# Attention and a wide MLP on one core: the fourth pair's products of v, its finish and the first MLP groups sit some cycles earlier, and the opening's loads go head by head

## The chip, the cores and the metric

The kernel runs on one core of a Trainium2 chip. The metric is the device time of one execution in microseconds (us). The engines are TensorE (PE in the profile, PEld for its weight loads), VectorE (DVE), ScalarE (ACT), GpSimd (POOL) and SyncE, whose queue (SPq) issues the DMAs. Each engine runs its own instructions strictly in order.

## What is computed

Attention over 8 batches of 8 heads, 576 positions and 64 dimensions, where only scores within tau of their row's maximum are kept; then an MLP over the 4608 rows of 512 features that come out, with 2048 hidden features and a slope of alpha below zero.

```python
scores = scale * np.matmul(q, k.transpose(0, 1, 3, 2))
thresh = np.max(scores, axis=-1, keepdims=True) - tau
scores = np.where(scores >= thresh, scores, -1000000000.0)
scores = scores - np.max(scores, axis=-1, keepdims=True)
attn = np.exp(scores)
attn = attn / (np.sum(attn, axis=-1, keepdims=True) + 1e-09)
attn_out = np.matmul(attn, v)
...
x = attn_out.transpose(0, 2, 1, 3).reshape(B * S, H * D)
h = x @ w_in
g = np.maximum(h, 0.0) + alpha * np.minimum(h, 0.0)
out = g @ w_out
```

The weights w_in and w_out arrive as float64; everything else is float32.

## The kernel before

**Pairs and cycles.** The 64 heads are worked in 32 pairs (class `Pair`), four to a batch. A pair has nine units of 128 queries, and each unit is one *cycle* of the main loop: 288 cycles for attention, pair `pi` in cycles `9*pi` to `9*pi+8`. In cycle i VectorE masks unit i and sums its rows (`mask`, L430), TensorE makes the scores two units ahead (`scores`, L395) and transposes unit i (`turn`, L439; `turn_k`, L455, and L453 for the fifth unit, the tail), ScalarE takes exponentials (`expo`, L418) behind VectorE's row maximum (`rowmax`, L410), and the transposed blocks are copied out of PSUM (`hi`, `lo`). Scores have two PSUM buffers.

**Beside the softmax.** Everything else of a pair hangs on a table of cycles: `at_cycle(i, f)` puts a step into cycle i, and the steps of a cycle run in the order in which they were put there. `PREP` places loads, splits and moves of q, k and v; `AVW` and `AVS` the four products of v (`avmul`, L542, copied out by `avout`, L553); `FINW` and `FINS` the seven steps of the finish: reciprocals of the row sums (`recip`, L560), their transpose (`rturn`, L565), a copy to `rt` that goes through DRAM and comes back spread over the rows as `rb` (`rout`, L569 to L574), the sum of v (`fin_add`), the multiply by `rb` (`fin_mul`, L589, POOL), a compare for rows that kept nothing (`fin_un`, L592, VectorE) and the last add with the store of x into `xs` (`fin_out`, L595 and L596). The first four pairs, which are batch 0, are worked whole (`WHOLE = 4`) and use the W tables, the others are split into high and low parts and use the S tables. For whole pairs each product is issued in two parts in neighbouring cycles. The numbers in the tables count from the pair's first cycle; `PREP` counts from the cycle nine earlier.

**The MLP beside attention.** Of the 16 blocks of 128 hidden features, seven (`F1`) are worked during attention, in groups of 256 rows (`Mlp`). A group is ready in cycle i once its rows' batches are finished, which a constant stands for:

```python
while nready < len(groups1) and sum(groups1[nready]) <= (i - RDY) // (9 * NPAIR) * S:
```

From then on `Mlp.cycle` gives TensorE work up to 2.6 us a cycle by its own count (`room`): first the load of x (L174, split by L180 on ScalarE and L182 on POOL one cycle later), then from the third cycle on *hidden blocks* (12 matmuls of line 194; L206 and L207 follow on VectorE and ScalarE), not in cycles that hold a product of v, then *output matmuls* (line 224). What is left when attention ends is done in the *drain*, in the scheduler's order, beside the decoding of the other nine blocks' weights (`Split64`, L113 to L152); then comes the last phase over all rows (`phb`, `accb`).

**Weights.** The float64 words are turned into two float32 parts by a chain over ScalarE, VectorE and POOL. The pieces of the seven blocks are decoded in cycles -3 to 40.

**Order.** Inside attention the order on TensorE, ScalarE, VectorE and POOL is the one in which the code issues; the order on SyncE's queue, and all orders after attention, are the scheduler's.

**Opening.** The first pair's k and q come doubled, in eight loads: all of k, then all of q; then tau, a first piece of w_in, the second pair's k and q. VectorE negates tau (L796) and then splits k and q for both heads (`prep_first`, L318 to L322).

Of the kernel before, what the change touches and what calls it, by code (L numbers as in the profile page):

```python
# [28 lines left out]
# A float64's upper word read as a float32 orders values by magnitude. These two  # L29
# bounds are the words of the least normal float32 and of the largest one that  # L30
# still rounds to a finite 12-bit part.
# [29 lines left out]
RDY = 13  # L61
# [8 lines left out]
def tile_masked_attention_moe(  # L70
# [31 lines left out]
    class Split64:  # L102
        """float64 bits -> hi + lo in float32r, to 24 bits or better."""
# [140 lines left out]
    class Turned:  # L244
        """The transposed scores of two heads, in parts, with columns of ones that sum v."""
# [21 lines left out]
    class Pair:  # L267
        """The steps of two heads of one batch; each queues work on one or two engines."""
# [8 lines left out]
        def load(self, what):  # L277
# [11 lines left out]
            if pi == 0:  # L289
                # The first pair's are doubled on the way in, so that its scores start at once.  # L290
                r = ap1.tile([P, KW if what == "k" else 2 * S], F32, tag="vst" if what == "k" else "p", name=f"{what}r{pi}", bufs=2)
                for j in range(2):
                    n = w if j else S
                    for half in range(2):
                        nc.sync.dma_start(r[half * D : (half + 1) * D, j * S : j * S + n], src[j * D : (j + 1) * D, :n])
                if what == "k":
                    self.kr = r
                else:
                    self.qr = r[:, : 2 * S].rearrange("p (a b) -> p a b", a=2)
                return  # L300
# [9 lines left out]

        def prep_first(self, j):
            """The splits of q and k for one head, before there is other work."""
# [11 lines left out]
        # The two heads' q and k come one above the other. The parts are made so, and then moved:  # L324
        # qst holds the parts of q one above the other, kh and kl each part of k twice.
# [51 lines left out]
        # A unit is (chunk of queries, head), or the tail: the last queries of the  # L377
        # first head above the first queries of the second.
# [225 lines left out]
    def first_at_cycle(i, fn):  # L604
        soon.setdefault(i, []).append((fn, ()))

    # Where in a pair's nine cycles the work beside the softmax falls.
    for p in pairs:
        o = 9 * p.pi
        n = o - 9  # L610
# [346 lines left out]
```

## Time and profile before

| | |
|---|---|
| three timed runs | 1399.51, 1401.48 and 1401.74 us; median 1401.48 |
| the profiled execution | span of 1397.3 us from the first to the last instruction; its time as a whole isn't listed apart |
| mean granted clock of TensorE | 0.995 |
| attention's last products of v | 829.16 us |
| the last phase's first matmul | 947.71 us |

Each row of the profile's order of time gives start and duration in us, engine, line, operation, tiles (out<-in), shapes and a count of merged instructions; in brackets the idle time of the engine ahead of it and what ended that. Rows of the chain of waits have start, duration and what worked. In the page, the first part gives busy time, share of the span and number of instructions of each engine.

### The profile page before, as it was taken

The page shows a single profiled execution, that of the slowest core. Times are in us where ns is not written, and L with a number is a line of the kernel's source. Part 1 is how long each engine was busy: PE and PEld are TensorE (multiplying, and loading weights), DVE is VectorE, ACT ScalarE, POOL GpSimd, SP SyncE. Part 2 cuts the span into 40 slices and gives each one's busy share as a digit, 9 for nine tenths or more (in the row PEclk, how much of TensorE's full clock was granted, in tenths as well). Part 3 has the DMA queues.
Part 4 walks back from the last instruction along what each step waited for, and adds up shares of the span by engine and source line. Part 5 has one row for each costly group of instructions (what it writes and reads, how often), then busy time and mean ns, then how long its engine had stood idle before and what let it go on. Part 6 is the DMA issues. An engine that isn't in the chain of part 4 may idle for free.

```text
span 1397.3 us, 23301 instructions
## 1 busy us (share of the span) xinstructions
PE 1339.4 (96%) x8116; PEld 1181.2 (85%) x8116; DVE 975.7 (70%) x1933; ACT 820.9 (59%) x1843; POOL 762.3 (55%) x821
## 2 busy tenths in 40 slices
PE   5888899999999999999999999888999999999998
PEld 4556789999999999999999998777888888888887
DVE  6999988888888898898888957986323323323332
ACT  7788888888888888888888854453112012111100
POOL 3776676666676666576676557566434124223311
PEclk9999999999999999999999999999999999999999
DMA  8643634545545444454454214433320220111011
GB/s 249 184 127 106 180 105 122 162 116 142 147 117 150 139 134 131 132 154 127 128 160 132 83 57 153 132 109 128 121 74 17 91 91 33 59 61 42 19 61 38
DMA packets 94628, 157.67 MB, mean 113 GB/s; under 512 B 14160, under 2 KB 39024, under 8 KB 94512
## 3 DMA queue, kind: packets, MB, share of 16 engines
q1 hardware_dynamic: 94512, 156.19, 38.4%
q8 instruction: 65, 1.06, 0.3%
q14 instruction: 51, 0.42, 0.1%
HBM read 85.53 MB, written 28.46 MB: 82 GB/s over the span
## 4 chain that ended last, share of the span: by engine, by line
PE 80%; DVE 9%; ACT 4%; DMA 2%; issue 2%; POOL 2%; SPq 0%; DVEq 0%; POOLq 0%; ACTq 0%
PE phb L194 16%; PE accb L224 16%; PE s L395 10%; PE av L542 10%; PE acca L224 9%; PE pha L194 9%; PE t L439 7%; DVE p L430 2%; DVE nmx L410 2%; DMA wri<-in_moe_w_in_dram 1%; PE tk L455 1%; DVE wti L135 1%; POOL wi L152 1%; ACT xb L555 1%; ACT xa L553 1%
## 5 line engine op out<-in xcount | busy, mean ns | idle before, releaser
L410 DVE TENSOR_REDUCE nmx<-s 128x1 f32<-128x576 f32 x288 | 217.0, 753 | 72.6 <-PE s L395 69.5
L215 ACT ACTIVATE gb<-ptb 128x512 fp32r<-128x512 f32 x81 | 50.9, 630 | 337.7 <-DVE ptb L873 337.3
L218 POOL TENSOR_TENSOR gb<-ptb,gb 128x512 fp32r<-128x512 f32 x81 | 104.4, 1290 | 257.0 <-ACT gb L215 256.8
L224 PE MATMUL acca<-wo,ga 128*128 128x512 f32 x756 | 230.7, 419 | 7.2 <-ACT ga L215 4.0
L224 PE MATMUL accb<-wo,gb 128*128 128x512 f32 x972 | 221.9, 389 | 0.0
L224 PEld LDWEIGHTS accb<-wo,gb 128*128 128x128 f32 x972 | 182.4, 188 | 37.9
L430 DVE SCALAR_TENSOR_TENSOR p<-s,thr,p 128x576 f32<-128x576 f32 x256 | 206.6, 807 | 1.3 <-ACT thr L423 0.9
L194 PE MATMUL phb<-xh,wi 128*128 128x512 f32 x648 | 202.9, 392 | 1.1 <-ACT xh L180 1.1
L194 PE MATMUL pha<-xh,wi 128*128 128x256 f32 x1008 | 199.7, 284 | 3.7 <-DVE pta L873 3.4
L418 ACT ACTIVATE p<-s,nmx 128x576 f32<-128x576 f32 x256 | 190.0, 742 | 10.8 <-DVE nmx L410 10.5
L395 PE MATMUL s<-kh,qst 128*128 128x288 f32 x640 | 142.2, 312 | 38.1 <-DVE p L430 23.3
L194 PEld LDWEIGHTS pha<-xh,wi 128*128 128x128 f32 x1008 | 163.8, 190 | 9.9 <-DVE pta L873 4.6
L224 PEld LDWEIGHTS acca<-wo,ga 128*128 128x128 f32 x756 | 132.8, 191 | 28.6 <-ACT ga L215 5.3
L439 PE MATMUL t<-ident,p 128*128 128x128 f32 x1024 | 154.6, 274 | 0.0
L395 PEld LDWEIGHTS s<-kh,qst 128*128 128x128 f32 x640 | 101.4, 193 | 61.5 <-issue 29.4
L903 DVE TENSOR_TENSOR ob<-accb,pin 128x512 f32<-128x512 f32 x36 | 24.2, 689 | 181.9 <-PE accb L224 181.9
L194 PEld LDWEIGHTS phb<-xh,wi 128*128 128x128 f32 x648 | 122.6, 189 | 27.2 <-ACT xh L180 1.5
L194 PE MATMUL pha<-xl,wi 128*128 128x256 f32 x504 | 142.2, 282 | 0.0
L872 DVE TENSOR_SCALAR ptb<-phb,alpha_sb 128x512 f32<-128x512 f32 x81 | 60.7, 751 | 108.5 <-PE phb L194 96.4
L395 PE MATMUL s<-kl,qst 128*128 128x288 f32 x640 | 133.8, 299 | 0.0
L194 PE MATMUL phb<-xl,wi 128*128 128x512 f32 x324 | 127.2, 393 | 3.6 <-POOL xl L182 3.6
L439 PEld LDWEIGHTS t<-ident,p 128*128 128x128 f32 x1024 | 126.5, 141 | 0.1
(117 smaller groups left out, 2772.6 us busy)
## 6 DMA issues: line engine op xcount, KB each, us to landing
kr<-in_k_dram SPq DMA_DIRECT2D x31, 320.0 KB
rb<-rvd SPq DMA_DIRECT2D x64, 144.0 KB
xs<-xa SPq DMA_DIRECT2D x32, 288.0 KB
part<-po SPq DMA_DIRECT2D x36, 256.0 KB
pin<-part SPq DMA_DIRECT2D x36, 256.0 KB
out_dram<-ob SPq DMA_DIRECT2D x36, 256.0 KB
vr<-in_v_dram SPq DMA_DIRECT2D x28, 320.0 KB
qr<-in_q_dram SPq DMA_DIRECT2D x31, 288.0 KB
```

The lines of the kernel that those rows point to most:

```text
L194: nc.tensor.matmul(ph[:, :n], w[:, c, :], xx[:, c, :n], start=(c == 0 and ti == 0), stop=(c == NCC - 1 and ti == 2),)
L215: nc.scalar.activation(g[:, 0, :n], t[:, :n], AF.Copy)
L218: nc.gpsimd.tensor_tensor(g[:, 1, :n], t[:, :n], f(g[:, 0, :n]), op=ALU.subtract)
L224: nc.tensor.matmul(acc[:m, :], gg[:, g, o : o + m], w, start=(first and ti == 0), stop=(last and ti == 2))
L395: nc.tensor.matmul(ps[:, h, :288], w, kk[:, a + h * 288 : a + (h + 1) * 288], start=(ki == 0 and i == 0), stop=(ki == 1 and i == n - 1),)
L410: nc.vector.tensor_reduce(self.nmx[:, j : j + 1], self.S[u][0][:, :, :288], axis=AX.XY, op=ALU.max, negate=True)
L418: nc.scalar.activation(pj, ps[:, :, :288], AF.Exp, bias=nmx[:, j : j + 1], scale=1.0)
L430: nc.vector.scalar_tensor_tensor(pj, ps[:, :, :288], thr[:, j : j + 1], pj, op0=ALU.is_ge, op1=ALU.mult, accum_out=self.sm[:, c : c + 1])
L439: nc.tensor.transpose(tb[:, c, :], pt[:, j, j * D + c * P : j * D + (c + 1) * P], ident)
L542: nc.tensor.matmul(pa[:m, :n], w, x, start=(part == 0 and c == 0), stop=(part == z.parts[-1] and c == NKC))
L872: nc.vector.tensor_scalar(t[:, :n], ph[:, :n], 0.0, alpha_sb[:, fc : fc + 1], op0=ALU.min, op1=ALU.mult)
L903: nc.vector.tensor_tensor(ob[:m], acc[:m], pi_[:m], op=ALU.add)
```

## The change

The fourth pair, the last of batch 0, gets tables of its own (`AVL`, `FINL`). Its products of v are issued whole, in cycles 32, 34, 36 and 37, where they stood in two parts each in cycles 32 to 39. The steps of its finish stay where they were up to `rout`; the sum of v moves three cycles forward, the multiply and the compare three, the last add and the store four: all three of the latter are in cycle 40. A group of the MLP is ready from seven cycles earlier in the first two batches' time (`RDY` 6 instead of 13) and three earlier after that (10). In the opening the loads go k, q of head 0, then k, q of head 1, and tau's negative stands behind the four splits. Comments are taken out, which shifts line numbers.

```diff
-RDY = 13
+AVL = (5, 7, 9, 10)
+FINL = (9, 10, 11, 11, 13, 13, 13)
+RDY = (6, 10)
...
             if pi == 0:
-                # The first pair's are doubled on the way in, so that its scores start at once.
-                r = ap1.tile([P, KW if what == "k" else 2 * S], F32, tag="vst" if what == "k" else "p", name=f"{what}r{pi}", bufs=2)
-                for j in range(2):
-                    n = w if j else S
-                    for half in range(2):
-                        nc.sync.dma_start(r[half * D : (half + 1) * D, j * S : j * S + n], src[j * D : (j + 1) * D, :n])
...
+                self.load_first()
                 return
...
+        def load_first(self):
+            self.kr = ap1.tile([P, KW], F32, tag="vst", name=f"kr{self.pi}", bufs=2)
+            qr = ap1.tile([P, 2 * S], F32, tag="p", name=f"qr{self.pi}", bufs=2)
+            self.qr = qr.rearrange("p (a b) -> p a b", a=2)
+            for j in range(2):
+                for r, src, w in ((self.kr, k, S + j * D), (qr, q, S)):
+                    for half in range(2):
+                        nc.sync.dma_start(
+                            r[half * D : (half + 1) * D, j * S : j * S + w], src[0, 0][j * D : (j + 1) * D, :w]
+                        )
...
         fin = FINW if p.whole else FINS
-        if p.whole:
+        if p.pi == NPAIR - 1:
+            fin = FINL
+            for c, step, j in zip(AVL, (0, 0, 1, 1), (0, 1, 0, 1)):
+                at_cycle(o + c, p.avmul, step, j)
+                at_cycle(o + c + 1, p.avout, step, j)
+        elif p.whole:
...
         p.load("k")
-        p.load("q")
         nc.sync.dma_start(tau_sb, tau.partition_broadcast(P))
-        nc.vector.tensor_scalar(ntau_sb, tau_sb, -1.0, None, op0=ALU.mult)
...
         p.prep_first(0)
         p.prep_first(1)
+        nc.vector.tensor_scalar(ntau_sb, tau_sb, -1.0, None, op0=ALU.mult)
...
-            while nready < len(groups1) and sum(groups1[nready]) <= (i - RDY) // (9 * NPAIR) * S:
+            while nready < len(groups1) and sum(groups1[nready]) <= (i - RDY[i >= 18 * NPAIR]) // (9 * NPAIR) * S:
```

What this does to the engines' orders, at three places. In the listings each row is a line, an operation and its tiles; after the change a line's number is 2 higher in the helpers (L127 is L129, L194 is L196) and 5 higher in the steps of `Pair` (L319 is L324, L430 is L435, L592 is L597).

VectorE's queue at the opening, before the change (`ntau_sb` is tau's negative, `kl` and `qst` the low parts of k and q, `wti` the first weight):

```order
L796 TENSOR_SCALAR ntau_sb<-tau_sb 128x1
L319 TENSOR_TENSOR kl_201<-kr_181,kh_200 128x576
L322 SCALAR_TENSOR_TENSOR qst_110<-qr_186,qst_110 64x576
L319 TENSOR_TENSOR kl_201<-kr_181,kh_200 128x640
L322 SCALAR_TENSOR_TENSOR qst_110<-qr_186,qst_110 64x576
L127 TENSOR_SCALAR wti_212<-wti_212 128x512
```

and with the change:

```order
L324 TENSOR_TENSOR kl_200<-kr_181,kh_199 128x576
L327 SCALAR_TENSOR_TENSOR qst_110<-qr_182,qst_110 64x576
L324 TENSOR_TENSOR kl_200<-kr_181,kh_199 128x640
L327 SCALAR_TENSOR_TENSOR qst_110<-qr_182,qst_110 64x576
L811 TENSOR_SCALAR ntau_sb<-tau_sb 128x1
L129 TENSOR_SCALAR wti_212<-wti_212 128x512
```

The negative moved from ahead of the splits to behind them, still ahead of the weight.

VectorE's queue around cycles 41 to 43, before the change; the compare of the fourth pair (`rb`) stands behind the masks of units 5, 6 and 7 of the fifth pair (`p_2`, `p_3`):

```order
L495 TENSOR_TENSOR eo_115<-t_3_1469,eo_114 128x4x128
L430 SCALAR_TENSOR_TENSOR p_2_1487,sm_1294<-s_5_1458,thr_5_1485,p_2_1487 128x576
L410 TENSOR_REDUCE nmx_5_1484<-s_6_1491 128x1
L495 TENSOR_TENSOR tt_121<-tk_t,tt_120 64x64
L495 TENSOR_TENSOR tt_123<-tk_t,tt_122 64x64
L495 TENSOR_TENSOR eo_115<-t_4_1498,eo_114 128x4x64 x2
L410 TENSOR_REDUCE nmx_7_1553<-s_7_1518 128x1
L430 SCALAR_TENSOR_TENSOR p_2_1487,sm_1294<-s_6_1491,thr_5_1485,p_2_1487 128x576
L495 TENSOR_TENSOR eo_115<-t_5_1526,eo_114 128x4x128
L430 SCALAR_TENSOR_TENSOR p_3_1556,sm_1294<-s_7_1518,thr_7_1554,p_3_1556 128x576
L410 TENSOR_REDUCE nmx_7_1553<-s_8_1560 128x1
L592 TENSOR_SCALAR rb_1448<-rb_1448,vs_1531 128x576
```

and with the change:

```order
L500 TENSOR_TENSOR eo_115<-t_3_1475,eo_114 128x4x128
L597 TENSOR_SCALAR rb_1451<-rb_1451,vs_1454 128x576
L435 SCALAR_TENSOR_TENSOR p_2_1491,sm_1296<-s_5_1464,thr_5_1489,p_2_1491 128x576
L415 TENSOR_REDUCE nmx_5_1488<-s_6_1495 128x1
L500 TENSOR_TENSOR tt_121<-tk_t,tt_120 64x64
```

The compare moved ahead of the mask of unit 5 (cycle 41).

TensorE's queue in cycle 49, before the change (`s` are scores, `t` and `tk_t` transposes, `av` a product of v):

```order
L395 MATMUL s_6_1783<-kh_1313,qst_111 128x288 x2
L395 MATMUL s_6_1783<-kl_1315,qst_111 128x288 x2
L439 MATMUL t_4_1794<-ident,p_t 128x128 x4
L453 MATMUL tk_t<-ident,p_t 64x128
L395 MATMUL s_7_1815<-kh_1313,qst_111 128x288 x2
```

and with the change:

```order
L400 MATMUL s_6_1823<-kh_1315,qst_111 128x288 x2
L400 MATMUL s_6_1823<-kl_1317,qst_111 128x288 x2
L444 MATMUL t_4_1834<-ident,p_t 128x128 x4
L458 MATMUL tk_t<-ident,p_t 64x128
L196 MATMUL pha_2_1848<-xh_0_1617,wi_462 128x256
L196 MATMUL pha_2_1848<-xl_0_1619,wi_462 128x256
```

A hidden block (`pha`) of the first group now stands in this cycle, and so in cycles 45 and 48. Counted over the whole order, the first hidden block is in cycle 45 instead of 52. Hidden blocks and output matmuls done by the end of a cycle, before and after: 0 and 0 against 3 and 0 (cycle 51); 7 and 0 against 10 and 9 (cycle 63); 16 and 64 against 17 and 84 (cycle 89); 21 and 84 against 21 and 84 (cycle 99); 93 and 512 against 93 and 514 (cycle 286). In cycles 98 and 99 the changed order has neither; before they had two blocks and three output matmuls. SyncE's queue has the store of the fourth pair's x and the first load of x (L174) ahead of a later pair's load of q and moves of k, where they stood behind those moves.

More of the change, by code (lines that the diff above doesn't have):

```diff
@@ L289, in load @@
             if pi == 0:
-                r = ap1.tile([P, KW if what == "k" else 2 * S], F32, tag="vst" if what == "k" else "p", name=f"{what}r{pi}", bufs=2)
-                for j in range(2):
-                    n = w if j else S
-                    for half in range(2):
-                        nc.sync.dma_start(r[half * D : (half + 1) * D, j * S : j * S + n], src[j * D : (j + 1) * D, :n])
[L296 to L299, printed above, removed]
+                self.load_first()
                 return
```

## The prediction

> **What bounds the kernel now.** I read the page first, then the windows, then the order of time around the change, then the chain.
>
> ```profile
> span 1397.3 us, 23301 instructions
> PE 1339.4 (96%) x8116; PEld 1181.2 (85%) x8116; DVE 975.7 (70%) x1933; ACT 820.9 (59%) x1843; POOL 762.3 (55%) x821
> ```
>
> The three timed runs have a median of 1401.48 us; the profiled execution has no time of its own beside its span of 1397.3, so I put 4.2 us around the span, work in microseconds of the span and carry the difference over to the median. TensorE is the bound as a whole, but not everywhere. The windows (from, to and length, then the busy times of the engines PE, PEld, DVE, ACT and POOL, the granted clock, DMA share, GB/s; the odd limits are the first transposes of cycles 32 and 38, 43 and 52, 98 and 100):
>
> ```profile
> 107.17:125.69 18.52, 16.20 (x88) 10.53 (x87) 18.40 (x35) 15.01 (x34) 13.52 (x11) 1.00 0.54 141
> 138.39:160.44 22.05, 16.38 (x124) 15.25 (x123) 20.17 (x45) 19.99 (x47) 11.15 (x11) 1.00 0.58 157
> 190.00:200.00 10.00, 7.93 (x47) 7.53 (x47) 7.57 (x20) 7.79 (x17) 6.64 (x7) 0.83 0.73 201
> 250.00:300.00 50.00, 50.00 (x367) 47.73 (x366) 44.19 (x99) 43.43 (x104) 32.76 (x42) 1.00 0.51 142
> 291.43:297.04 5.61, 5.61 (x46) 5.51 (x45) 5.51 (x14) 5.16 (x12) 3.54 (x6) 1.00 0.87 246
> 890.00:900.00 10.00, 7.49 (x35) 5.86 (x34) 9.71 (x13) 4.79 (x9) 8.39 (x7) 0.90 0.45 135
> ```
>
> From 200 to 825 us TensorE has no gap: work taken out there is time won, as far as VectorE (44.2 of 50) lets the cycles shrink. In cycles 43 to 51 VectorE and ScalarE are the fuller ones and TensorE has 22.05 - 16.38 = 5.67 us free; in cycles 32 to 37 VectorE is full (18.40 of 18.52). Around 890 us VectorE decodes the late weights and binds.
>
> **The change part by part.** *Opening.*
>
> ```profile
> 5.82 0.58 SPq L795 DMA_DIRECT2D tau_sb<-in_tau_dram  x1
> 6.81 0.68 ACT L321 ACTIVATE qst<-qr 128x576 fp32r<-128x576 f32 x1 [1.85 <-DMA qr<-in_q_dram]
> 9.09 0.15 DVE L796 TENSOR_SCALAR ntau_sb<-tau_sb 128x1 f32<-128x1 f32 x1 [9.09 <-DMA tau_sb<-in_tau_dram]
> 11.07 0.69 ACT L123 ACTIVATE wti<-wri 128x512 f32<-128x512 f32 x1 [2.29 <-DMA wri<-in_moe_w_in_dram]
> 12.41 0.43 DVE L127 TENSOR_SCALAR wti<-wti 128x512 f32<-128x512 f32 x1
> ```
>
> VectorE sat until tau landed at 9.09, with the splits of k and q queued behind it. Now the four splits stand ahead of tau's negative, and q of head 0 is issued two transfers (some 1.3 us) sooner. By these rows all four can be done by some 10 us instead of 12.4. Next in VectorE's queue is L127, which needs ScalarE's L123, and that waits for a weight load whose place in the queue is unchanged: it ends at 11.07 + 0.69 = 11.76. So what is late next is the weight, and the gain is 12.41 - 11.76 = 0.65 us, between 0 (swallowed by a later DMA wait) and 0.65. I take **-0.65**.
>
> *The fourth pair's products of v.* Its four products were issued in two parts each, in cycles 32 to 39; now each is issued whole, in 32, 34, 36 and 37.
>
> ```profile
> 126.22 1.84 PE L542 MATMUL av<-eo,vst 128*64 128x322 f32 x6
> 128.83 0.76 DVE L410 TENSOR_REDUCE nmx<-s 128x1 f32<-128x576 f32 x1 [1.18 <-PE s L395]
> ```
>
> The product of 322 columns that leaves cycles 38 and 39 has ten matmuls, 10 x 1.84 / 6 = 3.1 us. It lands in cycles 32 to 37, where TensorE has 18.52 - 16.20 = 2.3 us free: 0.8 us uncovered. Behind it VectorE's wait of 1.18 us for scores goes, of which I credit 0.5, since VectorE is the bound there. Bounds: -0.5 (all covered) and +3.1 (nothing is). I take **+0.3**.
>
> *Its finish.* The chain is reciprocal row, write, read back by rows, multiply (POOL), compare (VectorE), add (POOL), store, reload as x. The end of the last pair shows it with nothing in the way:
>
> ```profile
> 831.59 0.27 ACT L569 ACTIVATE rt<-rp 9x128 f32<-9x128 f32 x1
> 837.05 1.21 POOL L589 TENSOR_TENSOR xa<-xa,rb 128x576 f32<-128x576 f32 x1 [2.88 <-DMA rb<-rvd]
> 838.29 0.52 DVE L592 TENSOR_SCALAR rb<-rb,vs 128x576 f32<-128x576 f32 x1 [10.40 <-POOL xa L589]
> 840.13 0.32 SPq L596 DMA_DIRECT2D xs<-xa  x1
> 841.64 3.78 SPq L174 DMA_DIRECT2D xr<-xs  x3
> 841.64 5.87 DMA xr<-xs
> 125.12 0.27 ACT L569 ACTIVATE rt<-rp 9x128 f32<-9x128 f32 x1
> 131.03 0.81 DVE L430 SCALAR_TENSOR_TENSOR p<-s,thr,p 128x576 f32<-128x576 f32 x1
> 139.09 0.74 ACT L328 ACTIVATE kh<-kr 128x640 fp32r<-128x640 f32 x1
> 143.65 0.67 ACT L345 ACTIVATE qst<-qr 128x576 fp32r<-128x576 f32 x1
> ```
>
> From the row of reciprocals to the multiply are 837.05 - 831.59 = 5.46 us, to the compare 6.70, to the store 8.54, to the reload 10.05. Counted from the fourth pair's own row at 125.12 the compare can start at 131.82. In VectorE's order it now stands right ahead of the mask that started at 131.03, and that mask, the next row maxima and the transposes behind them queue after it: 0.79 us of stall; the compare's own 0.5 us only moves. The store comes at 133.66 and the reload's issue at 135.2; a load of 512 KB takes 4.42 us (the weight load below), so x is there at 139.6. ScalarE splits it right behind L328, which ends at 139.83: just in time. On SP's queue the reload now stands, with its wait for the store, ahead of a load of q, which goes out near 135.6 now; its reader (L345) ran at 143.65, so nothing waits. Bounds: 0, and 0.8 + 1.2 if the reload takes the 5.87 us that the chain has at 841.64. I take **+0.8**.
>
> *The feed-forward groups.* Cycles can be counted by the transposes: the tail's (L453) belongs to the fifth cycle of a pair, so 153.08 is in cycle 49. The order puts three hidden blocks (12 matmuls each) into cycles 45, 48 and 49, none into 58, nine output matmuls into 60 to 63 and a block into 63, where there was nothing.
>
> ```profile
> 142.27 0.50 PE L395 MATMUL s<-kh,qst 128*128 128x288 f32 x2 [0.77 <-DVE p L430]
> 145.41 0.50 PE L395 MATMUL s<-kh,qst 128*128 128x288 f32 x2 [1.93 <-DVE p L430]
> 153.08 0.27 PE L453 MATMUL tk_t<-ident,p_t 128*64 128x128 f32 x1
> 155.12 0.50 PE L395 MATMUL s<-kh,qst 128*128 128x288 f32 x2 [1.76 <-DVE p L430]
> 182.30 0.53 PE L395 MATMUL s<-kh,qst 128*128 128x288 f32 x2 [0.41 <-DVE p L430]
> 193.41 0.51 PE L395 MATMUL s<-kh,qst 128*128 128x288 f32 x2 [2.06 <-DVE p L430]
> 170.03 0.72 PE L542 MATMUL av<-o,vst 128*128 128x256 f32 x4
> 194.49 0.91 PE L542 MATMUL av<-o,vst 128*128 128x256 f32 x4
> 196.48 1.16 PE L395 MATMUL s<-kh,qst 128*128 128x288 f32 x4
> 202.44 1.44 PE pha L194 x12
> 830.76 6.38 PE acca L224 x28
> ```
>
> A hidden block is 1.44 us, an output matmul 6.38 / 28 = 0.23. In cycle 45 the block fits into the wait of 1.93. In 48 and 49 two blocks, 2.88 us, meet 1.76: 1.12 uncovered. In 60 to 63, 9 x 0.23 + 1.44 = 3.51 us meet 0.41 + 2.06: 1.04 uncovered; the block that leaves cycle 58 only lengthens the wait behind it. So the lead costs **+2.15**.
>
> It is paid back by cycle 103. The changed order has neither a block nor an output matmul in cycles 98 and 99; before they held two blocks and three output matmuls, 3.6 us. They took 5.61 us, and two cycles cannot go far below VectorE's pace, 22.05 / 9 = 2.45 us each in cycles 43 to 51: 5.61 - 4.9 = 0.7 us won there, and two new waits. Over the other cycles from 64 to 103 the counts of the order net to 2.0 us less (more output matmuls in the sixties and seventies, fewer in the nineties), where TensorE had no gap, and two output matmuls (0.46) stay ahead into the drain: **-3.2**. VectorE has the same steps, only earlier.
>
> *The clock.* Right behind the wait of 2.06 us the same product takes 0.91 us instead of 0.72, and the granted clock of 190 to 200 us is 0.83: 0.17 x 10 = 1.7 us lost. The block in cycle 63 fills that wait, so I count **-1.7**, between 0 and 1.7. The Trainium skill ("TensorE: Matmul & The Clock Gate", Part 1) has the clock halved only after an idle window of about 3.4 us; a wait of 2.06 us alone would not do it, and the sum would be -0.6 instead of -2.3. The trace has the slow rows right behind the wait, which bears my reading out, but waits of 1.93 and 1.76 us left the clock at 1.00, so the rule keeps a chance below.
>
> *The drain.* After attention the scheduler orders freely and has arranged blocks, weight decoding and loads differently.
>
> ```profile
> 868.02 4.42 DMA wri<-in_moe_w_in_dram
> 878.88 4.56 DMA wri<-in_moe_w_in_dram
> 947.71 7.36 PE phb L194 x21
> ```
>
> The chain runs there from a weight load to its decoding to the next load, 878.88 - 868.02 = 10.86 us a step, up to the last phase at 947.71. The same pieces are decoded; I put it at 0, with a load (4.4) fewer or a step (10.9) more as bounds.
>
> The sum: -0.65 + 0.3 + 0.8 + 2.15 - 3.2 - 1.7 = **-2.3**, so 1401.5 - 2.3 = 1399.2 us.
>
> **The rivals.** *Full cover:* cycles 48, 49 and 60 to 63 cost nothing, since two score buffers let TensorE run ahead: 2.15 less, 1397.0. For it speaks that VectorE has 22.05 - 20.17 = 1.9 us free in cycles 43 to 51, against it that it is VectorE's mask that TensorE waits for there and the blocks bring VectorE work of their own. *The clock dips all the same:* what closes it is not the one wait but the thin stretch around it, or the new waits at 98 and 99 close it there: 1399.2 + 1.7 = 1400.9. The Trainium skill's window, above, would read it so. *The drain saves a load:* 1399.2 - 4.4 = 1394.8; two pieces are decoded more closely interleaved on VectorE. *The drain takes one more step, slower:* place 837 to 948 us, price 10.9, so 1410.1; it decides from 5.1 us on, about half a step. For it: the changed order splits the last phase's first x (POOL) with four decoded pieces still behind it instead of three; against it: the same pieces, VectorE just as full. *The change doesn't do what it says:* x comes too late for cycle 43, ScalarE, which is in order, holds up the exponentials behind it, and the blocks start with a wait of their own. The feed-forward terms then give nothing, -0.65 + 0.3 + 2.0 = +1.65, 1403.1; for it the margin of 0.2 us above.
>
> **How the numbers follow.** A measurement here tells 0.2%, 2.8 us, from no change: the bounds are 1398.7 and 1404.3. Forecast 0.42, and as it ends so near the bound, 0.21 of it faster and 0.21 same; full cover 0.12, faster; clock 0.14, same; a load fewer 0.13, faster; a step more 0.12, slower; too late 0.07, of which 0.05 same and 0.02 slower. Faster 0.46, same 0.40, slower 0.14. The range takes in everything but the step more and the end of the load fewer: 1394.2 to 1404.0.
>
> **What would show it.** VectorE's first split near 5 us and L127 near 11.8. The first hidden block near 143 us, TensorE's free time in cycles 43 to 51 down from 5.7 to some 2.5, the granted clock of 190 to 200 us at 1.00, new waits of about 1.1 us in two cycles near 288 us; attention's last cycle some 2 us earlier, and the last phase's first matmul 2.3 us ahead of 947.71. A wait of VectorE's compare for POOL near 131 us of about 0.8 is right; one of 2 us or a wait of ScalarE's x split for its load makes the finish term wrong; a last phase that moves otherwise than attention's end makes the drain's zero wrong.

## The result and the profile after

| kernel | median of its runs, us | ratio to before, 95% interval |
|---|---|---|
| before | 1400.49 (4 runs, 1398.09 to 1401.74) | 1 |
| changed | 1416.66 (4 runs, 1411.42 to 1417.00) | 1.0108 [1.0091, 1.0124] |

The change makes the kernel 16.2 us slower; the forecast was 2.3 us faster, with 1404.0 as the upper end. Two executions of the experiments, one of the opening alone (1495.07 us at a granted clock of 0.85) and one of experiment 4 (3227.01 us at 0.42), were in a slow state and are left out of the medians and ratios below. The profiled execution of the changed kernel took 1416.35 us, with a span of 1414.6. The page:

```profile
span 1414.6 us, 23316 instructions
PE 1346.3 (95%) x8116; PEld 1187.9 (84%) x8116; DVE 977.3 (69%) x1933; ACT 821.5 (58%) x1843; POOL 761.7 (54%) x821
```

TensorE has the same 8116 matmuls but is busy 6.9 us longer: some of them ran slower. The rest of the 17.3 us that the span grew is waiting. The windows of the changed kernel, with the columns that the prediction explains; the odd limits are again the first transposes of cycles 32 and 38, 43 and 52, 98 and 100:

```profile
107.78:128.61 20.83, 18.31 (x99) 11.97 (x97) 19.55 (x36) 15.62 (x35) 14.45 (x14) 1.00 0.47 126
143.42:168.50 25.08, 22.08 (x160) 20.98 (x159) 21.05 (x48) 21.14 (x50) 15.75 (x19) 0.93 0.47 127
190.00:200.00 10.00, 9.83 (x74) 9.56 (x74) 8.66 (x21) 8.34 (x20) 8.19 (x7) 1.00 0.37 102
297.10:303.25 6.15, 3.00 (x19) 2.57 (x18) 5.56 (x13) 5.66 (x13) 3.70 (x5) 0.84 0.86 241
970.00:980.00 10.00, 1.92 (x5) 1.54 (x6) 7.64 (x13) 4.11 (x7) 5.06 (x4) 0.68 0.53 171
```

Cycles 32 to 37 grew by 20.83 - 18.52 = 2.3 us (the two behind them, which lose their product, give 1.3 back). In cycles 43 to 51 TensorE has 3.0 us free instead of 5.67, as wanted, but the stretch is 3.0 us longer. The clock of 190 to 200 us is 1.00, as forecast. In cycles 98 and 99 TensorE works 3.00 of 6.15 us. From 970 to 980 us it hardly works at all, where before it was in the last phase.

Where the time went can be read from the starts of the cycles (first transposes). The table gives how much longer each stretch took than in before, in us, and then the **rest**, the span less the start of cycle 287, for all kernels that are told of below. The first column measures little of the change: the opening alone and its variant with two output matmuls fewer (experiment 3), whose instructions are the same up to there, differ by 3.0 us in it; the clock of the first stood at 0.50 from 26.9 to 33.7 and from 71.2 to 74.6 us, that of the second didn't.

| kernel | cycle 0-36 | 36-45 | 45-63 | 63-99 | 99-108 | 108-287 | rest |
|---|---|---|---|---|---|---|---|
| before | | | | | | | 574.7 |
| changed | 1.9 | 4.8 | 2.7 | -3.3 | 3.2 | 1.4 | 581.7 |
| opening alone | 3.0 | -0.3 | 0.0 | -1.4 | 0.0 | -0.1 | 574.5 |
| opening, products | 2.3 | 0.0 | 0.0 | -1.4 | 0.0 | -0.2 | 574.3 |
| opening, products, finish ("pair") | 2.2 | 3.6 | 1.5 | -1.3 | 0.0 | -0.1 | 574.0 |
| pair, later batches at 10 | 2.1 | 4.1 | 1.5 | -1.0 | -0.5 | 1.3 | 575.8 |
| pair, first batch at 6 | 1.9 | 5.4 | 2.9 | -4.4 | 1.8 | 1.0 | 581.8 |
| pair, compare two cycles later | 4.0 | 0.9 | 1.2 | -1.3 | 0.0 | -0.1 | 575.5 |
| changed, transposes added in thin cycles | 2.3 | 3.0 | 2.9 | -2.6 | 1.2 | 1.3 | 581.7 |

Two places carry the loss: some 10 us in attention, most of it between cycles 36 and 108, and 581.7 - 574.7 = 7.0 us behind it, in the drain.

**The finish.** The order of time of the changed kernel around cycle 40, by engine:

```profile
127.94 0.27 ACT L574 ACTIVATE rt<-rp 9x128 f32<-9x128 f32 x1
129.49 1.10 SPq L579 DMA_DIRECT2D rb<-rvd  x2
133.27 1.21 POOL L594 TENSOR_TENSOR xa<-xa,rb 128x576 f32<-128x576 f32 x1 [3.18 <-DMA rb<-rvd]
132.08 0.68 DVE L500 TENSOR_TENSOR eo<-t,eo 128x512 fp32r<-128x512 f32 x1
134.51 0.52 DVE L597 TENSOR_SCALAR rb<-rb,vs 128x576 f32<-128x576 f32 x1 [1.75 <-POOL xa L594]
132.11 0.50 PE L400 MATMUL s<-kh,qst 128*128 128x288 f32 x2 [1.82 <-DVE p_t L435]
135.82 0.85 PE L400 MATMUL s<-kh,qst 128*128 128x288 f32 x2 [2.40 <-DVE p L435]
```

From the row of reciprocals to the multiply are 133.27 - 127.94 = 5.33 us (the prediction took 5.46), but VectorE is at the compare at 132.76 and waits 1.75 us for it. The mask behind it comes late, and TensorE waits 2.40 us for the mask. Its next matmuls are slow too: the two of the scores take 0.85 us instead of 0.50.

**The thin cycles.** The same in cycles 98 and 99, where no block stands any more, and the windows behind them:

```profile
299.36 0.50 PE L400 MATMUL s<-kh,qst 128*128 128x288 f32 x2 [1.55 <-DVE p L435]
302.16 0.82 PE L400 MATMUL s<-kh,qst 128*128 128x288 f32 x2 [1.60 <-DVE p L435]
300.00:302.00 2.00, 0.56 (x5) 0.32 (x3) 1.97 (x6) 1.91 (x4) 0.39 (x1) 0.81 0.89 221
304.00:306.00 2.00, 2.00 (x7) 1.65 (x6) 1.83 (x5) 1.44 (x4) 1.89 (x2) 0.50 0.23 46
306.00:308.00 2.00, 2.00 (x10) 1.87 (x9) 0.05 (x1) 0.14 (x1) 0.00 (x0) 0.50 0.75 198
```

TensorE's clock is 0.50 while TensorE is busy all the time, and from 306 us on the other engines have next to nothing to do. Cycle 100 takes 3.2 us longer than in before.

**The drain.** TensorE's waits behind attention, in the changed kernel (engine, line, what it waited for, total, times, longest):

```profile
PE phb L196 <- DVE ptb L882: 8.5, 1, 8.5
PE phb L196 <- POOL xl L184: 4.3, 1, 4.3
```

The second wait stood in before too (3.56 us ahead of the row at 947.71). The first is new: the last phase, once begun, stops for 8.5 us. What it waits for can be followed on POOL, whose joins of decoded weights (L154, in before L152) free the buffers for the next loads. First the changed kernel, with the issue of the load that is held up, two rows of VectorE and the window behind TensorE's wait, then before, with the issue of the same load:

```profile
949.14 1.32 POOL L154 TENSOR_TENSOR wo<-wto,wro 128x512 fp32r<-128x512 f32 x1 [0.68 <-POOL wto L151]
950.41 4.68 POOL L184 TENSOR_TENSOR xl<-xr,xh 128x2048 fp32r<-128x2048 f32 x1
957.54 1.80 POOL L151 TENSOR_TENSOR wti<-wti,wi 128x512 f32<-128x512 f32 x1 [0.43 <-DVE wri L142]
962.83 1.30 POOL L154 TENSOR_TENSOR wo<-wto,wro 128x512 fp32r<-128x512 f32 x1 [3.48 <-DVE wto L151]
964.08 1.31 POOL L154 TENSOR_TENSOR wi<-wti,wri 128x512 fp32r<-128x512 f32 x1
974.25 1.40 POOL L154 TENSOR_TENSOR wi<-wti,wri 128x512 fp32r<-128x512 f32 x1 [8.86 <-DVE wti L151]
964.15 0.37 SPq L115 DMA_DIRECT2D wri<-in_moe_w_in_dram  x1
968.68 0.43 DVE L129 TENSOR_SCALAR wti<-wti 128x512 f32<-128x512 f32 x1 [5.93 <-ACT wti L125]
974.43 1.40 DVE L881 TENSOR_SCALAR ptb<-phb,alpha_sb 128x512 f32<-128x512 f32 x2
978.00:984.00 6.00, 5.92 (x14) 4.67 (x15) 3.42 (x6) 3.10 (x4) 3.33 (x3) 0.51 0.55 189
```

```profile
941.68 1.31 POOL L152 TENSOR_TENSOR wi<-wti,wri 128x512 fp32r<-128x512 f32 x1
942.95 4.71 POOL L182 TENSOR_TENSOR xl<-xr,xh 128x2048 fp32r<-128x2048 f32 x1
952.23 1.71 POOL L152 TENSOR_TENSOR wo<-wto,wro 128x512 fp32r<-128x512 f32 x1 [2.56 <-DVE wto L149]
956.31 1.31 POOL L152 TENSOR_TENSOR wi<-wti,wri 128x512 fp32r<-128x512 f32 x1
943.02 0.38 SPq L113 DMA_DIRECT2D wri<-in_moe_w_in_dram  x1
```

In before the last but one piece of w_in is joined right ahead of the 4.7 us split of x, 119.1 us behind the start of cycle 287 (822.57). In the changed kernel that piece comes behind the split, and its join stands in POOL's queue behind a join of w_out that waits 3.48 us for VectorE: 131.2 us behind the start of cycle 287 (832.90). The last load of w_in is issued only then: 131.25 us behind the start of cycle 287 (964.15), against 120.45 in before (943.02). VectorE, waiting 5.93 us for it, takes up the last phase's `ptb` only behind the decoding, at 974.43, and TensorE, whose PSUM buffers `ptb` frees, stops until then. Its first 6 us behind the wait run at a granted clock of 0.51, so a part of the drain's loss is the clock's.

The loss stands behind the point where the last phase begins. Counted from the start of cycle 287, its first matmul behind the split of x comes after 122.25 us in the changed kernel (955.15) and after 125.14 in before (947.71); three matmuls of that phase in before (from 941.54) and four in the changed kernel (from 948.63) run ahead of the split. So the drain is 2.9 us shorter up to there, and what follows is 9.9 us longer.

### The profile page after: what moved, and what is told of

It reads as the page before. It is cut to its first block, busy times and chain, and to the rows that moved or that the text cites. A ratio compares the mean times of both kernels' runs of the same rounds, so it can differ in the third digit from the quotient of the medians.

```text
span 1414.6 us, 23316 instructions
## 1 busy us (share of the span) xinstructions
PE 1346.3 (95%) x8116; PEld 1187.9 (84%) x8116; DVE 977.3 (69%) x1933; ACT 821.5 (58%) x1843; POOL 761.7 (54%) x821
## 4 chain that ended last, share of the span: by engine, by line
PE 79%; DVE 10%; ACT 5%; issue 2%; DMA 2%; POOL 1%; SPq 0%; DVEq 0%; POOLq 0%; ACTq 0%
PE accb L226 16%; PE phb L196 15%; PE av L547 11%; PE s L400 10%; PE pha L196 9%; PE acca L226 9%; PE t L444 7%; DVE p L435 2%; DVE nmx L415 1%; PE tk L460 1%; DMA wro<-in_moe_w_out_dram 1%; DVE wto L137 1%; ACT xh L182 1%; ACT xb L560 1%; DMA wri<-in_moe_w_in_dram 1%
## 5 line engine op out<-in xcount | busy, mean ns | idle before, releaser
L226 PE MATMUL acca<-wo,ga 128*128 128x512 f32 x756 | 227.5, 417 | 4.9 <-ACT ga L217 2.3
L196 PE MATMUL phb<-xh,wi 128*128 128x512 f32 x648 | 205.3, 395 | 8.7 <-DVE ptb L882 8.5
L435 DVE SCALAR_TENSOR_TENSOR p<-s,thr,p 128x576 f32<-128x576 f32 x256 | 206.8, 808 | 1.5 <-ACT thr L428 1.1
L196 PE MATMUL pha<-xh,wi 128*128 128x256 f32 x1008 | 200.4, 284 | 5.2 <-DVE pta L882 5.0
L196 PEld LDWEIGHTS pha<-xh,wi 128*128 128x128 f32 x1008 | 163.9, 190 | 11.8 <-DVE pta L882 6.3
L444 PE MATMUL t<-ident,p 128*128 128x128 f32 x1024 | 156.9, 277 | 0.0
L196 PEld LDWEIGHTS phb<-xh,wi 128*128 128x128 f32 x648 | 123.8, 191 | 35.9 <-DVE ptb L882 8.9
L196 PE MATMUL pha<-xl,wi 128*128 128x256 f32 x504 | 142.1, 282 | 0.0
L196 PE MATMUL phb<-xl,wi 128*128 128x512 f32 x324 | 128.2, 396 | 4.3 <-POOL xl L184 4.3
```

Of the source, the lines that this page charges most:

```text
L196: nc.tensor.matmul(ph[:, :n], w[:, c, :], xx[:, c, :n], start=(c == 0 and ti == 0), stop=(c == NCC - 1 and ti == 2),)
L226: nc.tensor.matmul(acc[:m, :], gg[:, g, o : o + m], w, start=(first and ti == 0), stop=(last and ti == 2))
L435: nc.vector.scalar_tensor_tensor(pj, ps[:, :, :288], thr[:, j : j + 1], pj, op0=ALU.is_ge, op1=ALU.mult, accum_out=self.sm[:, c : c + 1])
L444: nc.tensor.transpose(tb[:, c, :], pt[:, j, j * D + c * P : j * D + (c + 1) * P], ident)
```

## The experiments

Beside each median stands that of before, taken in the same group of runs. The edits are given against the changed kernel. RDY holds the cycles by which the groups of the first and of the later batches become ready; 13 for both is before.

**1. One part at a time.** Opening alone: RDY = (13, 13), and the fourth pair with before's tables AVW and FINW.

> The opening's loads and tau's negative alone; products, finish and feed-forward groups as before. The drain's order is the same as before here. All theories: 0.3 to 0.65 us less than before (cycle 9 starts 0.30 us sooner in the changed kernel), some 1400 us; a difference that only the clock's dip near 70 us could turn to +0.6.

The pair (products and finish) without any early group:

```diff
-RDY = (6, 10)
+RDY = (13, 13)
```

> Opening and the fourth pair's products and finish forward; the groups become ready as before (13). Theory A (stalls at the finish, and the clock halved behind the thin stretches they make, between cycles 38 and 51): cycle 54 starts 3 to 6 us later than before, attention ends as much later. Theory B (the drain's order): the drain's order is neither kernel's here, so span less attention's end differs from the 555.9 us of before by several us either way. Theory C (the early feed-forward blocks themselves cost): attention ends within 1 us of before, since no block is early here.

The first batch early, RDY = (6, 13):

> As changed, but only the first batch's two groups are ready early (6); the later batches' as before (13). Attention up to cycle 108 has the changed kernel's order. Theory A and C alike: attention ends some 10 us later than before, as in the changed kernel. Theory B: the drain differs from the changed kernel's, and its length (span less attention's end, 563 us there) with it; if the drain is not the cause of the last 7 us, it is 563 again.

The later batches early, RDY = (13, 10):

> Opening and fourth pair as changed, the first batch's groups ready as before (13), the later ones at 10. Theory A: the same loss as in the run of the pair without early groups up to cycle 72; theory C: none. Theory B: the drain has VectorE's and POOL's order of before here, so span less attention's end is before's, 555.9 us within 1, and the total is that of the pair's loss alone.

Measured, beside before's 1400.97 us: opening 1398.92 (0.9991 [0.9977, 1.0004]), pair 1403.90 (1.0022 [1.0012, 1.0031]), first batch early 1413.76 (1.0089 [1.0074, 1.0104]), later batches early 1406.16 (1.0036 [1.0023, 1.0049]). So some 10 us come with the first batch's early groups, 5.0 with the pair, and 2 to 3 with the later batches (1406.16 - 1403.90, or 1416.66 - 1413.76). The column "rest" splits the 10: the drain is 574.0 in the run of the pair and 581.8 with the early groups, though these stand some 700 us ahead of it. The theory that only stalls in attention count falls here, and so does the one that only the drain counts.

Two of the expectations had the drain's order wrong. By the traces the order of operations behind the start of cycle 287 on POOL, VectorE and ScalarE is before's in the run of the pair, and the changed kernel's in that of the first batch early; so these two runs don't separate the early groups from the drain's order. Experiment 3 does.

The opening alone also bears on the prediction's clock term. Its order is before's in cycle 63, without a block. The last two rows are from its variant with two output matmuls ahead (experiment 3), with the same order there:

```profile
195.93 0.51 PE L400 MATMUL s<-kh,qst 128*128 128x288 f32 x2 [2.05 <-DVE p L435]
190.00:200.00 10.00, 7.92 (x62) 7.39 (x62) 8.82 (x20) 8.90 (x21) 8.10 (x9) 1.00 0.74 195
195.42 0.51 PE L400 MATMUL s<-kh,qst 128*128 128x288 f32 x2 [2.08 <-DVE p L435]
190.00:200.00 10.00, 7.90 (x51) 7.49 (x50) 8.13 (x19) 8.39 (x20) 8.06 (x9) 0.83 0.80 205
```

In the opening alone the wait is there (2.05 us), the clock stays at 1.00, and cycles 63 to 99 are 1.4 us shorter all the same; in the variant the clock dips. Nine of the sixteen traces have this wait unfilled (2.05 to 2.08 us), and three of them dip at it (before, this variant, and the run ready at 11 below); of the six in which cycle 63 has its block, none does (the sixteenth, ready at 10, has two waits of 1.5 us there and dips). So the dip doesn't follow from the wait: without the block it came in one trace of three. Whether the block also keeps it away isn't shown.

**2. Products or finish, and how early the groups must be.** Products forward, finish as before:

```diff
-            fin = FINL
-RDY = (6, 10)
+RDY = (13, 13)
```

> Opening and the fourth pair's products forward, its finish where it was (14, 16, 16, 17), groups ready at 13; the drain's order is before's. If the finish (the compare that waits for POOL, and the clock behind it) makes the pair's 4.5 us: total within 1.5 us of the opening alone (1399.4), no stretch at half clock between 125 and 160 us. If the bunched products make it: 1403 to 1404, as with the finish.

Measured 1401.13 us beside 1400.29 (1.0010 [0.9999, 1.0021]), 0.2 us outside what was expected; cycles 36 to 63 as in before, no stretch at half clock there. The products cost some 1 us (cycles 32 to 39 are 0.96 us longer here, 0.97 in the changed kernel). By the cycles the finish makes the rest of the pair's loss (36 to 45: 0.0 here, 3.6 in the pair); by the totals alone it isn't clear of noise, since the two intervals overlap.

RDY = (11, 10) and RDY = (10, 10). With 11 the scheduler has POOL and VectorE work through the drain as in before, with 10 in the changed kernel's kind of order; by cycle 280 the latter is one output matmul further (498 against 497):

> As changed, the first batch's groups ready at 11 (instead of 6); the scheduler then gives VectorE and POOL before's order in the drain. Drain theory: span less the last cycle's transposes is 575 to 576 us, as in the runs with before's order; total 1405 to 1408. Rival, that early groups make the drain longer by what they leave over: between 576 and 582.

> As changed, ready at 10: a single cycle sooner than in the run at 11, and the scheduler gives VectorE and POOL the changed kernel's kind of order in the drain. Drain theory: span less the last cycle's transposes is 580 to 583 us, total some 6 us more than the run at 11 with an attention that ends within 2 us of it. Rival, that the length follows how early the groups are: both runs differ by under 1.5 us in the drain.

Measured 1407.31 (1.0046 [1.0028, 1.0064]) and 1412.74 (1.0091 [1.0070, 1.0111]); rest 575.2 and 581.1 us, cycle 287 at 830.80 and 830.12. One cycle in the time at which a group becomes ready is worth 5.9 us in the drain.

**3. The drain by itself.** A counter-test from both sides. The changed kernel, with two output matmuls held back at the end of attention, so that the drain starts with before's leftover and gets its order:

```diff
             used += busy.get(i, 0.0)
+            if i == 284:
+                used += 0.45
```

> The changed kernel with 0.45 us more counted as used in cycle 284, so that two output matmuls of the first phase stay for the drain, as in before; the scheduler then gives the drain before's order on VectorE and POOL. Attention as changed (ends 10 us late). Drain theory (the order that follows from what is left over costs some 6 us): span less the last cycle's transposes is 575 to 576.5 us instead of 581.7, total 1409.5 to 1411.5. Rival, that the early groups leave a longer drain whatever its order: 580 to 582, total 1415 to 1417.

The opening alone, with two output matmuls done ahead (the same lines with -0.45), and with two fewer (+0.25):

> The opening alone, with 0.45 us less counted as used in cycle 284: two output matmuls more are done in attention, none of the change's other parts. The scheduler then gives VectorE and POOL the changed kernel's order in the drain. Drain theory: span less the last cycle's transposes is 580 to 583 us instead of 574.5, total 1405 to 1407. Rival, that the order of the drain is harmless and the early groups make the 7 us: 574 to 575, total 1399 to 1400.

> The opening alone, with 0.25 us more counted as used in cycle 284: two output matmuls fewer in attention. The drain's order is a third one, in which POOL joins each piece of w_in ahead of the piece of w_out that follows, as in before. Drain theory: 573 to 576 us, total 1398.5 to 1401. Rival, that any other leftover than before's makes the drain longer: 578 or more, total above 1403.

Measured beside 1400.36 us: held back 1409.24 (1.0063 [1.0048, 1.0078], 0.3 us below what was expected), rest 576.4; ahead 1406.38 (1.0039 [1.0026, 1.0051]), rest 581.0; fewer 1399.32 (0.9986 [0.9974, 0.9998]), rest 574.8. With two output matmuls ahead and nothing else, the wait of the last phase and POOL's order are those of the changed kernel:

```profile
PE phb L196 <- DVE ptb L884: 9.2, 1, 9.2
942.36 4.68 POOL L184 TENSOR_TENSOR xl<-xr,xh 128x2048 fp32r<-128x2048 f32 x1
954.77 1.31 POOL L154 TENSOR_TENSOR wo<-wto,wro 128x512 fp32r<-128x512 f32 x1 [3.48 <-DVE wto L151]
956.04 1.32 POOL L154 TENSOR_TENSOR wi<-wti,wri 128x512 fp32r<-128x512 f32 x1
```

With them held back, the changed kernel has before's:

```profile
951.98 1.31 POOL L154 TENSOR_TENSOR wi<-wti,wri 128x512 fp32r<-128x512 f32 x1
953.24 4.71 POOL L184 TENSOR_TENSOR xl<-xr,xh 128x2048 fp32r<-128x2048 f32 x1
```

So the drain's 7 us are shown: they come of the order that the scheduler makes from what attention leaves over. The sixteen traces agree. Nine kernels (before, the opening, its products, the pair, the later batches, ready at 11, held back, and those of experiments 4 and 6) have the same order on POOL, VectorE and ScalarE behind the start of cycle 287, 238 output matmuls behind attention's last transpose, and a rest of 574.0 to 576.4 us. Six (changed, first batch early, ready at 10, two ahead, and both of experiment 5) share another order there, 236 or 237 output matmuls, and a rest of 581.0 to 582.9. The variant with two fewer has a third order, 239 output matmuls, and 574.8. One or two output matmuls, 0.23 us each, decide which. What in the slow order costs the time was read from the rows above and not taken apart by an edit: the split of x stands ahead of four joins in it and of three in the two others, but more differs between them.

**4. The stall.** The pair, RDY = (13, 13), with the compare on VectorE, and POOL's add and the store behind it, two cycles later; the multiply stays:

```diff
-FINL = (9, 10, 11, 11, 13, 13, 13)
+FINL = (9, 10, 11, 11, 13, 15, 15)
```

> Opening and the fourth pair's products and finish forward, groups ready at 13, as in the run of the pair (1403.9), but the finish's compare on VectorE and POOL's add and store two cycles later (15 instead of 13; the multiply stays at 13). Stall theory (the compare, queued ahead of the mask, waits for POOL's multiply, which waits for the reciprocals' way through memory): no wait of VectorE for POOL near 133 us, cycle 45 starts within 1 us of its place in the run with the products alone, total 1400 to 1402. Rival, that the pair's loss comes of the finish's work in cycles that are full anyway: cycle 45 as late as in the run of the pair, total 1403 to 1404.5.

```profile
139.45 0.50 DVE L597 TENSOR_SCALAR rb<-rb,vs 128x576 f32<-128x576 f32 x1
```

The compare waits for nothing, and TensorE's wait of over 2 us for the mask behind it is gone. Cycles 36 to 45 take 0.9 us more than in before instead of 3.6, and the median is 1401.96 beside 1400.36 (1.0015 [1.0004, 1.0026]) instead of the pair's 1403.90 (1.0022 [1.0012, 1.0031]). The rows and cycles bear the stall theory out; the totals point the same way, but their intervals overlap. What stays are 0.9 us and two stretches at half clock (136.2 to 139.6 and 146.4 to 153.2 us).

**5. The clock.** Six transposes of the identity a cycle, into columns of the score buffer that nobody reads, right behind the cycle's own transposes, where TensorE would wait; the other engines' order stays. First in cycles 39 to 47, 98 and 99:

```diff
             do(i, "turn_k")
+            p, u = unit(i + 2)
+            for c in range(FILL.get(i, 0)):
+                nc.tensor.transpose(p.S[u][:, c % 2, 288:416], ident, ident)
```

> The changed kernel with six transposes of the identity (some 0.66 us), into columns of the score buffer that nobody reads, behind the transposes of cycles 39 to 47, 98 and 99; they change no result and no order on the other engines. Clock theory (TensorE's clock is halved for whole windows of 3.4 us where it was mostly idle in the window before): the stretches at half clock at 134-141, 147-151 and 301-308 us, which lose 3.40 + 1.71 + 3.42 = 8.5 us, go for the most part, attention ends 4 to 8 us sooner, total 1408 to 1413. Rival, that the waits cost the time and the clock is beside it: the stalls at cycle 40 and 98, 99 stay, attention ends within 1 us of the changed kernel's or up to 3 us later, total 1415 to 1420.

Measured 1417.70 beside 1400.29 (1.0120 [1.0103, 1.0136]): no gain, as the rival had it, though behind 50 us only one of attention's stretches at half clock was left, near 70 us. Cycles 45 to 63 lost 4.5 us instead of 2.7, which may be the added work in cycles that were full, so this run decides nothing. Once more, in cycles 39 to 41, 98 and 99 alone:

> The changed kernel with six transposes of the identity in cycles 39, 40, 41, 98 and 99 only, where TensorE waits. No stretch at half clock at 134-141 and 301-308. If the clock is a cause: of the 4.8 us lost from cycle 36 to 45 and the 3.2 us from 99 to 108 some 2 to 3 and 2 to 3 us go, and the total is 1411 to 1414. Rival, that the waits alone set it: 4 to 5 and 3 us again, total 1416 to 1418.

Measured 1413.59 beside 1399.46 (1.0094 [1.0071, 1.0117]); the medians point down, but the interval holds the changed kernel's 1.0108. The cycles say more: 36 to 45 lose 3.0 us instead of 4.8, 99 to 108 lose 1.2 instead of 3.2, though cycles 98 and 99 themselves get 1.0 us longer with the added work. The same matmuls of the scores as above, behind a wait that is as long, and the window:

```profile
302.54 0.50 PE L401 MATMUL s<-kh,qst 128*128 128x288 f32 x2 [1.68 <-DVE p L436]
304.00:306.00 2.00, 2.00 (x15) 1.82 (x14) 1.63 (x5) 1.47 (x4) 1.22 (x1) 1.00 0.43 104
```

A second trace agrees: the kernel with two output matmuls held back has the changed kernel's instructions up to cycle 284, its clock stayed at 1.00 from 290 to 320 us, and its cycles 99 to 108 took 0.4 us more than before's instead of 3.2. So the clock is a part of the cause: by these two traces 1.8 us at the first place, and at the second (cycles 98 to 107) 1.2 us net of the added work, or 2.8 by the second trace. What stays there are the waits.

**6. Finish, drain and later batches put right, the first batch's groups still early.** They are ready at 8 here, 6 in the changed kernel and 13 in before; the later batches are as in before.

```diff
-FINL = (9, 10, 11, 11, 13, 13, 13)
-RDY = (6, 10)
+FINL = (9, 10, 11, 11, 13, 15, 15)
+RDY = (8, 13)
+            if i == 284:
+                used += 0.25
```

> The changed kernel with the compare, add and store two cycles later (15), the first batch's groups ready at 8, the later batches' at 13 as before, and 0.25 us more counted as used in cycle 284, so that the drain starts with before's leftover and has before's order. If stall, drain and later batches are all of the loss but for some 2 us of the early groups (2.2 us more at attention's end in the run with early groups than in that of the pair): span less the last cycle's transposes 574 to 576, total 1402 to 1405. If the early groups alone cost more than that: 1406 or more. If they gain once the failures are gone: below 1400.

Measured 1403.06 beside 1399.46 (1.0025 [1.0013, 1.0037]), rest 575.0: the first case of the expectation. Cycles 45 to 63 lose 4.9 us, with a stretch of 7 us at half clock in them, and 63 to 99 give back 4.1. Even then no gain from the early groups can be seen: the kernel without them and with the same finish (experiment 4) had 1.0015.

## Why the prediction missed, point by point

The step that failed is the last term: "**The drain.** ... The same pieces are decoded; I put it at 0". It measured +7.0 us, the largest single part of the 16, in a kernel whose attention was two output matmuls further at its end. That the same pieces are decoded was right; that their order doesn't matter was the assumption that failed, and experiment 3 showed the order to decide. The rival "the drain takes one more step, slower" had the sign and the step: the last load of w_in goes out 131.25 - 120.45 = 10.8 us later, near its price of 10.9, and 7.0 of them reach the end. Its place, 837 to 948 us, was wrong: up to the last phase's first matmul behind the split the drain is 2.9 us shorter, and the loss comes behind it. Its argument for itself, that the split of the last phase's first x stands ahead of four decoded pieces instead of three, fits every trace, but isn't tested apart from the rest of the order. It got 0.12 where the order that was in hand spoke for it.

Terms of attention failed too, the finish by more than its bound:

- **Opening, -0.65.** VectorE's first split starts at 5.02, as forecast, and L129 (L127 before) at 12.13 instead of 11.8. In time: 0.9991 of before, -1.3 us, with an interval from -3.2 to +0.6. Not refuted, not shown.

```profile
5.02 0.76 DVE L324 TENSOR_TENSOR kl<-kr,kh 128x576 fp32r<-128x576 f32 x1 [5.02 <-ACT kh L323]
12.13 0.43 DVE L129 TENSOR_SCALAR wti<-wti 128x512 f32<-128x512 f32 x1 [2.06 <-ACT wti L125]
```

- **Products, +0.3.** +0.97 in cycles 32 to 39 of the changed kernel; within its bounds.
- **Finish, +0.8.** Mis-sized: +3.4 in cycles 40 and 41. The chain's length was right; its start was taken from before's row at 125.12. The bunched products made cycles 32 to 37 longer, so it started at 127.94; then cycles 38 and 39 lost their products and 1.3 us, and VectorE was at the compare 1.7 us later than assumed, the chain 2.7. The stall is 1.75 instead of 0.79. And what hangs on it was left out: TensorE's wait of 2.40 us and the half clock behind it (1.8 us by the second run of experiment 5). The x split came as assumed, without a wait for its load, but its 1.04 us on ScalarE stands ahead of an eviction and an exponential, and cycle 44 is 1.44 us longer, with a stretch at half clock from 147.6 to 151.0 us (0.95 us in the second run of experiment 5, without that stretch):

```profile
144.76 1.04 ACT L182 ACTIVATE xh<-xr 128x1024 fp32r<-128x1024 f32 x1
145.83 0.60 ACT L496 ACTIVATE eo<-t 128x512 fp32r<-128x512 f32 x1
148.24 0.82 PE L400 MATMUL s<-kh,qst 128*128 128x288 f32 x2 [1.72 <-DVE p L435]
```

- **Groups' lead, +2.15, paid back -3.2.** The changed kernel less the run of the later batches alone: 7.5 - 5.6 = +1.9 in cycles 36 to 63, and -3.3 + 1.0 = -2.3 in 63 to 99. The run of the first batch early less that of the pair gives +3.2 and -3.1. Both are near. But for cycles 98 and 99 the sum had "0.7 us won there, and two new waits" without a price: cycles 99 to 108 are 3.7 us longer than in that run, 1 us of it without the clock (the second trace in experiment 5).
- **Clock, -1.7.** The dip at 194 us did go, but it is gone in the opening alone too, without the block. The term counted as sure what came in three of nine traces (experiment 1), so its coming true was in part luck. And four other dips came in attention, two of them twice as long. The rival "the clock dips all the same" named cycles 98 and 99 as the place; it did not have the finish, and priced a single dip.
- **Later batches** had no term: 2 to 3 us, by the run at 10 against that of the pair 1.7 in attention and 1.9 behind it.

"The change doesn't do what it says" is out, since x came in time and TensorE's free time in cycles 43 to 51 did fall; the two faster rivals are out by the sign.

## What to carry to other kernels

Where a scheduler orders a later stage by what an earlier one leaves over, a small move upstream can reshuffle it as a whole: compare the orders there, and price what stands ahead of the joins that free the load buffers, before writing 0. A short step that waits for a memory round trip belongs where its input is surely there, since in an engine that is in order everything behind it pays, and so does the engine that waits for that. Work moved forward from a later stretch leaves that stretch thin, which has a price of its own.

## What the hardware showed that was not expected

TensorE's clock is lost in portions. Summed in steps of 0.5 us, the granted clock missing from full speed was 1.7, 3.4 or 5.1 us in every dip behind 50 us of the sixteen traces, but for the one that the end of the span cuts off: one, two or three stretches of 3.4 us at 0.50. The dips came where TensorE was busy in the 3.5 us ahead for 0 to 1.9 us; the wait right ahead could be as short as 1.6 us (302.16 above), and a wait of 2.05 us could leave the clock alone (195.93 above). The Trainium skill ("TensorE: Matmul & The Clock Gate", Part 1) has a free-running window of 3413 ns, and the portions agree with it; it has the clock halved after an idle window, and here most dips came behind 3.5 us in which TensorE was busy for a third to a half. That the window's phase is chance isn't shown by itself, but fits the scatter of one and the same order of instructions: the opening alone and its variant with two output matmuls fewer differ in nothing before cycle 284, and their cycles 45 to 63 were 0.0 and 3.8 us longer than in before, the second with two dips (143.3 to 150.1 and 156.9 to 160.3 us). So a few us of attention between two single traces of this kernel can be chance, those of the table above too, where no row or second trace stands beside them; the drain's 6 to 7 us are beyond that, by the two groups of experiment 3.
